# Weight chunk, small loads and tail transposes issued at other places in the start of an attention-plus-ReGLU kernel

## The chip, the cores and the metric

The kernel runs on one core of a Trainium2 chip. The metric is the device time of one execution in microseconds. Times differ a little from run to run and between chips, so every kernel was timed in turns with the kernel before on the same chip. The profile shows one of the executions, and its span is some 1.7 us shorter than the time of the same run. That execution need not be a typical one: the profiles of the kernel after, e5, e8, e9 and e10 fell on the fastest run of their kernel, those of e2, e6 and e7 on the slowest. Where a time in microseconds is given beside a ratio, the ratio is the one to trust.

## The reference, cut to what matters

```python
# q, k, v: (8, 8, 576, 64); beacon_k, beacon_v: (8, 8, 16, 64): 16 extra keys seen by every query
scores = scale * np.matmul(q, k_all.transpose(0, 1, 3, 2))      # causal on the 576 own keys
a = softmax(scores)
x = (a @ v_all) reshaped to (4608, 512)
out = (np.maximum(x @ w_gate, 0) * (x @ w_val)) @ w_out         # 512 -> 1536 -> 512
```

So there are eight batches of attention, then a feed-forward part over 4608 rows. The kernel runs them interleaved: TensorE does scores and e·v of one batch between the matmuls of the feed-forward part for rows that are ready.

## The kernel before

Everything is planned on the host as a list of steps. Steps one to seven are batch one alone, then come four steps without attention, of which three do feed-forward work, then batch two. Actions are hung on a step: `between` (behind the first score matmuls), `mid` (behind the first exponential), `behind`, and `after` (at the end). Each engine runs what it is given in this order. In the code, batches and steps count from 0 and `s2` is 11, the first step of batch two.

```python
def load_rows(self, srcs, held=False):
    raw = self.raw["rows"] = stage.tile([P, d_model], FP32, name="raw")
    n = srcs.shape[1]
    if held:
        nc.gpsimd.memset(raw[:1, :1], 0.0)     # SyncE's load below must wait for GpSimd to get here
    nc.sync.dma_start(...)
...
mid[3] = lambda: load_w(wg, moe_w_gate, 256, 768, (0,))
after(3, lambda: load_w(wg, moe_w_gate, 256, 768, (1,)))
...
after(6, lambda: load_w(wv, moe_w_val, 256, 768))          # GpSimd, float32 to bf16 on the way
after(6, load_small)                                       # beacon, key tail, query tail of batch two
for n0 in (768, 1152):
    after(6, lambda n0=n0: load_w(wg, moe_w_gate, n0, n0 + 384))
    after(6, lambda n0=n0: load_w(wv, moe_w_val, n0, n0 + 384))
after(6, lambda: load_second(0))                           # four "quarters" (hwide) of batch two, GpSimd
after(7, lambda: load_second(1))                           # four more
for t in range(NKT):
    after(7, lambda t=t: second.load("v", t, t == 0))      # SyncE; v block 0 is held by a memset
for t in range(NKT):
    after(s2 - 1 + t // 2, lambda t=t: second.cast("v", t, pool))
after(s2 - 2, lambda: load_wo(0, 6))                       # GpSimd, 768 KB as landed
after(s2 - 1, lambda: load_wo(6, 12))
after(s2 - 3, lambda: cast_small(second))                  # VectorE casts the three small loads
after(s2 - 2, lambda: turn_small(second))                  # TensorE transposes them
mid[s2 - 1] = lambda: turn_two(second, 0, s_ps)            # TensorE transposes the first four quarters
between[s2 + 1] = lambda: turn_two(second, 1, f_ps)
```

Names, for the timelines below: `wg`, `wv` and `wo` are the gate, value and output weights, and L466, L475 and L485 their matmuls; `hT` is the product of gate and value that L485 reads. `e` holds exponentials (L378, ScalarE), GpSimd masks them (L386), and L420 is e·v. `raw` buffers take float32 rows from memory, and a cast brings them to bf16 (`half`, `hwide`). A quarter (`hwide`) is 256 rows of q or k for four of the eight heads; the tails are the last rows, which the quarters leave out. A hold is a memset by GpSimd that a load must wait for; a hole is time in which TensorE stands idle. The granted clock is the share of full speed that TensorE was allowed, 1.0 or 0.5.

## Time and profile before

| what | value | where it is read |
|---|---|---|
| time | 397.75 us median (397.14 to 399.54, 4 runs) | timed runs |
| span of the profile | 396.4 us | page |
| TensorE busy | 374.1 us, 94% | page, part 1 |
| first feed-forward matmul (L466) | 29.68 us | timeline |
| GpSimd's first issue of a 768-column chunk | 30.29 us | timeline |
| GpSimd's memset that opens the v hold | 46.64 us | timeline |
| cast of batch two's first v rows starts | 57.10 us | timeline |
| TensorE resumes with e·v of batch two | 59.73 us | timeline |

The timeline: start us, duration, engine, line, what it does, and in brackets how long the engine had stood idle and what released it. The prediction below shows the lines themselves.

### The profile page before, as it was taken

Reading aid. Unit: us, or ns where it says so; the run is one execution under the profiler, and the core shown is the slowest. Engines: PE = TensorE matmul, PEld = TensorE weight load, DVE = VectorE, ACT = ScalarE, POOL = GpSimd, SP = SyncE. Lnnn points to the kernel's source line nnn. Section 1 sums busy time; section 2 is a strip of 40 time slices with the busy share of each in tenths; the row PEclk is TensorE's granted clock in tenths of the full one; section 3 lists DMA queues with packets and bytes.
Section 4 is the critical chain, followed back from the end, with each engine's and each line's share of the span. In section 5 each row is a group of like instructions: output and inputs, shape, how many; then the busy total and the mean of one; then the engine's idle time right before and its main releaser. Section 6 shows DMA issues by size and latency. Waiting matters only on the chain.

```text
span 396.4 us, 10219 instructions
## 1 busy us (share of the span) xinstructions
PE 374.1 (94%) x4243; PEld 189.8 (48%) x4299; DVE 204.9 (52%) x344; ACT 192.2 (48%) x268; POOL 127.7 (32%) x221
## 2 busy tenths in 40 slices
PE   7889669999999999999999999999999999999995
PEld 3464334544455445544454545554555454444443
DVE  4685435644556756366636564556555654421320
ACT  4663155533755655455636653656365643322321
POOL 1577526521653445053505350526020200000000
PEclk9999698999999999999999999999999999999999
DMA  8969999967989999399629962796210011002002
GB/s 217 196 121 163 188 201 190 208 146 160 207 157 156 208 186 133 103 200 173 124 96 198 181 122 96 179 189 135 71 53 2 2 55 53 2 27 81 1 25 86
DMA packets 148131, 50.43 MB, mean 127 GB/s; under 512 B 133616, under 2 KB 143600, under 8 KB 148080
## 3 DMA queue, kind: packets, MB, share of 16 engines
q1 hardware_dynamic: 139024, 44.48, 54.9%
q0 software_dynamic: 9056, 5.24, 10.0%
q8 instruction: 35, 0.57, 0.6%
q14 instruction: 16, 0.13, 0.1%
HBM read 38.34 MB, written 9.44 MB: 121 GB/s over the span
## 4 chain that ended last, share of the span: by engine, by line
PE 72%; DMA 13%; issue 5%; SPq 4%; POOL 3%; ACT 1%; DVE 1%; POOLq 0%; ACTq 0%
PE f L485 19%; PE f L466 19%; PE s L475 11%; PE f L475 8%; PE s L370 6%; PE ab L420 6%; DMA raw<-in_q_dram 4%; DMA raw<-in_v_dram 4%; DMA raw<-in_k_dram 3%; PE os L420 2%; DMA kT<-half 2%; SPq L244 2%; SPq L281 1%; ACT e L378 1%; SPq L310 1%
## 5 line engine op out<-in xcount | busy, mean ns | idle before, releaser
L378 ACT ACTIVATE e<-s 128x1024 bf16<-128x1024 f32 (+2 forms) x112 | 104.9, 963 | 27.4 <-PE s L370 27.4
L466 PE MATMUL f<-xT,wg 128*128 128x512 bf16 x405 | 110.3, 383 | 2.3 <-DMA hwide<-in_k_dram 0.7
L469 ACT ACTIVATE g<-f 128x512 f32<-128x512 f32 x108 | 64.6, 598 | 87.7 <-PE f L466 78.8
L485 PE MATMUL f<-wo,hT 128*128 128x512 bf16 (+1 forms) x424 | 94.8, 373 | 1.6 <-issue 0.8
L386 POOL TENSOR_SCALAR_AFFINE_SELECT e<-e 128x512 bf16<-128x512 bf16 (+2 forms) x80 | 47.3, 603 | 150.7 <-ACT e L378 142.4
L432 DVE RECIPROCAL r<-os 128x80 f32<-128x80 f32 (+2 forms) x43 | 57.6, 1339 | 56.5 <-PE os L420 56.5
L477 DVE TENSOR_TENSOR hT<-g,s 128x512 bf16<-128x512 f32 x60 | 41.3, 688 | 69.0 <-PE s L475 67.9
L475 PEld LDWEIGHTS <-wv 128*128 128x128 bf16 x432 | 42.6, 99 | 53.1 <-issue 3.4
L485 PEld LDWEIGHTS <-hT 128*128 128x128 bf16 x444 | 41.9, 98 | 47.3
L466 PEld LDWEIGHTS <-wg 128*128 128x128 bf16 x432 | 39.7, 98 | 47.6 <-issue 2.1
L475 PE MATMUL s<-xT,wv 128*128 128x512 bf16 x238 | 62.3, 383 | 0.2
L488 ACT COPY ob<-f 128x512 f32<-128x512 f32 (+1 forms) x37 | 21.3, 575 | 73.9 <-PE f L485 69.1
L477 DVE TENSOR_TENSOR hT<-g,f 128x512 bf16<-128x512 f32 x48 | 33.0, 688 | 35.3 <-PE f L475 30.6
L475 PE MATMUL f<-xT,wv 128*128 128x512 bf16 x186 | 49.0, 381 | 0.7 <-ACT qT L301 0.2
L263 POOL CAST half<-raw 128x512 bf16<-128x512 f32 (+2 forms) x60 | 37.1, 633 | 25.3 <-DMA raw<-in_k_dram 9.3
L420 PE MATMUL ab<-e,v 128*32 128x80 bf16 (+4 forms) x1320 | 39.7, 235 | 3.4 <-POOL e L386 3.4
L370 PE MATMUL s<-qT,kT 64*128 64x80 bf16 (+3 forms) x704 | 36.0, 236 | 1.8 <-ACT e L378 1.1
L420 PEld LDWEIGHTS <-v 128*32 128x32 bf16 (+1 forms) x1408 | 26.7, 98 | 13.3 <-issue 7.9
L370 PEld LDWEIGHTS <-kT 64*128 64x128 bf16 x704 | 20.5, 97 | 25.8 <-issue 23.6
L420 PE MATMUL os<-e,ones 128*32 128x240 bf16 (+4 forms) x660 | 32.3, 234 | 0.0
L259 POOL CAST v<-raw 128x512 bf16<-128x512 f32 (+1 forms) x39 | 25.6, 662 | 15.1 <-DMA raw<-in_v_dram 14.4
L445 DVE TENSOR_TENSOR xT<-ab,r 128x480 bf16<-128x480 f32 (+2 forms) x45 | 25.0, 554 | 0.8
(68 smaller groups left out, 139.0 us busy)
## 6 DMA issues: line engine op xcount, KB each, us to landing
out_dram<-ob SPq DMA_DIRECT2D x35, 256.0 KB, 2.1
raw<-in_q_dram SPq DMA_DIRECT2D x25, 256.0 KB, 4.8
raw<-in_v_dram SPq DMA_DIRECT2D x24, 256.0 KB, 5.0
raw<-in_k_dram SPq DMA_DIRECT2D x19, 256.0 KB, 4.4
raw<-in_v_dram SPq DMA_DIRECT2D x8, 224.0 KB, 3.8
wo<-in_moe_w_out_dram POOLq DMA_DIRECT2D x2, 768.0 KB, 9.5
raw<-in_k_dram SPq DMA_DIRECT2D x6, 224.0 KB, 4.3
raw<-in_v_dram SPq DMA_DIRECT2D x8, 160.0 KB, 4.3
```

The costliest lines, as they stand in the source:

```text
L259: copy(self.v[:n, t].rearrange("p (h a d) -> p h a d", a=2, d=C), raw[:n].rearrange("p (h d a) -> p h a d", a=2, d=C))
L263: copy(h[:n], raw[:n])
L370: nc.tensor.matmul(self.s[:, a, c + j * n:c + (j + 1) * n], kT[rows, 2 * g + j, k0:k0 + P], qT[rows, 2 * g + j, q0:q0 + n], start=True, st ...
L378: nc.scalar.activation(e[:, :k * 4 * n].rearrange("p (k a x) -> p a k x", k=k, a=2), self.s[:, :, :k * 2 * n].rearrange("p a (k x) -> p a ...
L386: nc.gpsimd.affine_select(out=cols[:, :, :m], in_=cols[:, :, :m], pattern=[[0, 4], [1, m]], compare_op=ALU.is_ge, fill=0.0, base=base, cha ...
L420: nc.tensor.matmul(o[:, q0 - cq0:q0 - cq0 + n], w, e[:kr, 2 * (hh % 2) + hh // 2], start=(i == 0 and part != 1), stop=(i == self.last), sk ...
L432: nc.vector.reciprocal(self.r[:, :n], self.os[:, :n])
L466: nc.tensor.matmul(g[:, :n], wg[:, ki, nf * P:(nf + 1) * P], x[:, ki], start=(ki == 0), stop=(ki == KM - 1))
L469: nc.scalar.activation(gs[:, :n], g[:, :n], AF.Relu)
L475: nc.tensor.matmul(u[:, :n], wv[:, ki, nf * P:(nf + 1) * P], x[:, ki], start=(ki == 0), stop=(ki == KM - 1))
L477: nc.vector.tensor_mul(self.h[:, nf, c0:c1], gs[:, :n], u[:, :n])
L485: nc.tensor.matmul(o[:, n], self.h[:, nf, ms * P:(ms + 1) * P], wo[:, nf, n], start=(nf == 0), stop=(nf == NF - 1))
```

## The change

The intent: the second 256-to-768 chunk of the value weights is issued from the fourth step on, the small loads of batch two go without a hold, and the tails of batch one (its last 80 rows) are cast and transposed later, in a score bank, so that the copies of the last quarters need not wait for them. Some casts change engine to make room. The diff, with the dead `held` parameter of `load_rows` cut:

```diff
         def turn_next():
             turn_first("k", 0, 1, dve)()
             first.cast_quarter("k", 1, 0, dve)
-            warm_up(1, 256)
...
             held.pop()()
-            warm_up(1, 256)
             turn_first("k", 1, 0, dve)()
...
         def cast_last():
             for n in "kq":
                 first.cast_quarter(n, 1, 1, dve)
+
+        def turn_last():
+            for n in "kq":
+                turn_first(n, 1, 1, dve)()
             cast_tails(first, dve)
 
         def turn_first_tails():
-            ps = f_ps.tile([P, 2, NP, 80], BF16, name="f")
+            ps = s_ps.tile([P, 2, NP, 256], BF16, name="s")
...
-        between[2] = lambda: [turn_first(n, 1, 1, dve)() for n in "kq"]
-        behind[2] = turn_first_tails
-        after(2, lambda: [held.pop(0)() for _ in range(2)])
-        after(2, lambda: first.cast("v", 2, pool))
-        after(2, lambda: first.cast("v", 3, pool))
-        mid[3] = lambda: load_w(wg, moe_w_gate, 256, 768, (0,))
-        after(3, lambda: load_w(wg, moe_w_gate, 256, 768, (1,)))
-        after(4, lambda: first.cast("v", 4, dve))
-        after(4, lambda: cast_w(wg, raw_g, 256, 0, dve))
-        after(4, lambda: cast_w(wg, raw_g, 256, 1, pool))
-        after(5, lambda: cast_w(wv, raw_v, 256, 0, pool))
-        after(6, lambda: cast_w(wv, raw_v, 256, 1, pool))
-        after(6, lambda: load_w(wv, moe_w_val, 256, 768))
-
-        def load_small():
-            second.beacon = second.load_rows(beacon_k[1], True)
-            load_tails(second)
-
-        after(6, load_small)
+        between[2] = turn_last
+        between[3] = turn_first_tails
+        behind[3] = lambda: [held.pop(0)() for _ in range(2)]
+        after(1, lambda: first.cast("v", 2, pool))
+        after(1, lambda: first.cast("v", 3, pool))
+        mid[3] = lambda: load_w(wg, moe_w_gate, 256, 768)
+        after(3, lambda: load_w(wv, moe_w_val, 256, 768, (0,)))
+        after(4, lambda: first.cast("v", 4, pool))
+        mid[5] = lambda: [cast_w(wg, raw_g, 256, g, pool) for g in range(2)]
+        mid[6] = lambda: load_w(wv, moe_w_val, 256, 768, (1,))
+        after(6, lambda: [cast_w(wv, raw_v, 256, g, act) for g in range(2)])
+        second.beacon = second.load_rows(beacon_k[1])
+        load_tails(second)
```

More of the change, by code (lines that the diff above doesn't have):

```diff
@@ L303, in turn_quarter, with load_rows @@
                 ps.rearrange("a j r p -> a j p r"))
-        def load_rows(self, srcs, held=False):
+        def load_rows(self, srcs):
             raw = self.raw["rows"] = stage.tile([P, d_model], FP32, name="raw")
             n = srcs.shape[1]
-            if held:
-                nc.gpsimd.memset(raw[:1, :1], 0.0)
             nc.sync.dma_start(raw[:n].rearrange("p (h d) -> p h d", d=D),
@@ L630, in cast_last @@
                 first.cast_quarter(n, 1, 1, dve)
+        def turn_last():
+            for n in "kq":
+                turn_first(n, 1, 1, dve)()
             cast_tails(first, dve)
         def turn_first_tails():
-            ps = f_ps.tile([P, 2, NP, 80], BF16, name="f")
+            ps = s_ps.tile([P, 2, NP, 256], BF16, name="s")
             for x, (h, dst) in enumerate(zip(first.tails, (first.kT4, first.qT4))):
-                held.append(first.turn_rows(h, dst[:, :, :80], act, ps[:, x]))
+                held.append(first.turn_rows(h, dst[:, :, :80], act, ps[:, x, :, :80]))
         behind[1] = cast_last
-        between[2] = lambda: [turn_first(n, 1, 1, dve)() for n in "kq"]
-        behind[2] = turn_first_tails
-        after(2, lambda: [held.pop(0)() for _ in range(2)])
-        after(2, lambda: first.cast("v", 2, pool))
-        after(2, lambda: first.cast("v", 3, pool))
-        mid[3] = lambda: load_w(wg, moe_w_gate, 256, 768, (0,))
-        after(3, lambda: load_w(wg, moe_w_gate, 256, 768, (1,)))
-        after(4, lambda: first.cast("v", 4, dve))
-        after(4, lambda: cast_w(wg, raw_g, 256, 0, dve))
-        after(4, lambda: cast_w(wg, raw_g, 256, 1, pool))
-        after(5, lambda: cast_w(wv, raw_v, 256, 0, pool))
-        after(6, lambda: cast_w(wv, raw_v, 256, 1, pool))
-        after(6, lambda: load_w(wv, moe_w_val, 256, 768))
-        def load_small():
-            second.beacon = second.load_rows(beacon_k[1], True)
-            load_tails(second)
-        after(6, load_small)
+        between[2] = turn_last
[11 more added lines that the diff above has]
+        load_tails(second)
         for n0 in (768, 1152):
```

## The prediction

> **What bounds the kernel now.** I read the page first, for the shape of the whole run. In the page's 40 slices (9.9 us each) TensorE is full from the seventh on; the clock and DMA rows show where it is not.
>
> ```profile
> PE   7889669999999999999999999999999999999995
> PEclk9999698999999999999999999999999999999999
> DMA  8969999967989999399629962796210011002002
> ```
>
> Count digits: PE has 6, 6 in slices 5 and 6 (39.6 to 59.5 us), the clock has 6 and 8 in slices 5 and 7. DMA has its one early dip, a 6, in slice 3 (19.8 to 29.7 us), and is at 9 right after. So what the change can win lies before 64 us; after that the list of TensorE waits for 64 to 396 us holds only 1.0 us, all "issue". Anything gained early should reach the end, if the later transfers keep up.
>
> Next, the busy time by stretch, whose last three columns are granted clock, DMA share and GB/s:
>
> ```profile
> 21.00:24.00 3.00, 2.90 (x70) 1.97 (x65) 2.02 (x6) 2.22 (x3) 2.99 (x6) 1.00 0.43 95
> 24.00:30.00 6.00, 4.29 (x200) 3.42 (x201) 5.29 (x13) 3.77 (x5) 3.83 (x7) 1.00 0.60 86
> 36.00:42.00 6.00, 4.32 (x20) 1.84 (x19) 1.95 (x6) 1.20 (x2) 2.49 (x4) 1.00 1.29 197
> 42.00:50.00 8.00, 5.93 (x52) 3.38 (x53) 4.40 (x14) 1.20 (x2) 4.39 (x7) 0.58 1.68 185
> ```
>
> From 21 to 30 us DMA moves 86 to 95 GB/s, then 185 to 197. The queue is saturated in one stage and half empty in the stage before it. Third, the timeline around the TensorE holes:
>
> ```profile
> 16.02 0.46 DVE L317 CAST half<-raw 80x512 bf16<-80x512 f32 x1 [0.26 <-DMA raw<-in_q_dram]
> 17.13 0.69 PE L325 MATMUL f<-ident,half 80*128 80x80 bf16 x8 [1.26 <-DVE kT L301]
> ...
> 38.18 0.42 DVE L317 CAST half<-raw 64x512 bf16<-64x512 f32 x1 [1.25 <-DMA raw<-in_k_dram]
> 41.40 0.42 DVE L317 CAST half<-raw 64x512 bf16<-64x512 f32 x1 [2.79 <-DMA raw<-in_q_dram]
> 42.50 0.60 ACT L469 ACTIVATE g<-f 128x512 f32<-128x512 f32 x1 [4.14 <-DVE hT L477]
> 43.15 0.78 PE L325 MATMUL f<-ident,half 16*128 16x16 bf16 x12 [2.83 <-ACT g L469]
> 46.29 1.91 PE L475 MATMUL s<-xT,wv 128*128 128x512 bf16 x4
> ...
> 57.10 1.20 POOL L259 CAST v<-raw 128x512 bf16<-128x512 f32 x2 [9.60 <-DMA raw<-in_v_dram]
> 58.26 0.82 POOL L350 DMA_DIRECT2D wo<-in_moe_w_out_dram  x1
> 59.08 0.60 POOL L386 TENSOR_SCALAR_AFFINE_SELECT e<-e 128x448 bf16<-128x448 bf16 x1
> 59.73 0.39 PE L420 MATMUL ab<-e,v 128*32 128x240 bf16 x8 [3.12 <-POOL e L386]
> ```
>
> Three holes. **First**, at 15.9 to 17.1 us TensorE waits for VectorE, which sat waiting for the tails of batch one. **Second**, at 40.2 to 43.2 us: batch two's small rows (key tail, query tail) are late, VectorE waits for them in order, so the hT products behind them are late, ScalarE has no g buffer, and TensorE has no bank. Four matmuls then take 1.91 us instead of 1.03. **Third**, at 56.6 to 59.7 us: TensorE waits for a mask on GpSimd that stands behind the cast of batch two's first v rows, and that cast waited 9.60 us for its transfer. Fourth view, the queue of issues:
>
> ```profile
> SPq L244 <- POOL raw L241: 14.6, 1, 14.6
> SPq L310 <- POOL raw L309: 10.8, 1, 10.8
> ```
>
> SyncE stood still for 10.8 us before the small loads and 14.6 us before v, because a one-element GpSimd memset holds each buffer. The small loads could have gone at 19.4 us, when SyncE's last weight issue ended.
>
> **What the Trainium skill says.** "DMA: Bandwidth & Descriptors", Issuing engines are not separate DMA queues: transfers issued anywhere run on the same 16 engines and interleave. The trace agrees: the 128 KB query tail, issued by SyncE at 31.48 us among GpSimd's weight chunks, took 9.9 us. "TensorE: Matmul & The Clock Gate", Architectural detail: VectorE and ScalarE queues are strictly first in, first out. The trace agrees: the hT product at 41.74 us runs only behind the 2.79 us wait of L317. The same page, What's actually happening: an idle TensorE falls to half clock after an idle window of about 3.4 us. The trace shows the fall after holes of 2.9 and 3.1 us; granted clock 0.58 in 42 to 50 us. "Perfetto Trace Analysis", DMA Instruction — SWDGE: a GpSimd DMA's row ends with descriptor generation, not with the data. So I read landings from the DMA issues in narrow windows: the 0.72 us rows land 4 to 10 us after issue.
>
> **The change part by part.**
>
> Tails of batch one. Their casts leave the place ahead of the kT and qT copies (0.67 + 0.67 us at 16.40 and 17.00), and their transposes get a score bank one step later. The two transposes of the last quarters end near 15.1 us, so the copies can run at about 15.0 to 16.3 and the first e·v group at about 15.8 (after the score matmuls of 15.26) instead of 17.74; v rows 0 and 1 were cast by 15.48. The eight tail transposes (0.6 us) come back in step four, and ScalarE's two tail copies (0.43 + 0.43) now stand between two exponentials. ScalarE then does one exponential per 1.02 us; following it from 17.45, the last one ends at about 27.1 instead of 28.31. Gain here: about **1.2 us**. The warm-up matmuls taken out (two of 0.4 us) filled time in which TensorE waited for VectorE casts; I give them 0.
>
> Casts moved. v block 4 and one wg half go from VectorE (0.41 each) to GpSimd (0.62 each), both wv halves from GpSimd (0.61 each) to ScalarE after its last exponential (0.62 each, its row for a cast of this shape). They end near 28.4, before wv is first read at about 29.4. GpSimd's total hardly moves: 0.
>
> Weight chunk two. The first half of wv[256:768] is issued at about 23.6 and the second at about 27.3, instead of both at 28.82. Each is 256 KB, in time for their use at about 32.8 (a lone one landed in 4.0 us).
>
> Small loads. 32 + 128 + 128 KB move from 30.4 us to 19.5. So 0.29 + 0.26 MB leave the saturated stretch; at about 190 GB/s (the narrow windows: 192 KB chunks land 1.0 us apart) that is 2.9 us. And GpSimd starts the stream earlier: its first 768-column wg issue goes from 30.29 to about 28.1, as it has 1.2 us from the exponentials, and two wv issues fewer but one at 27.3 there. By landings: that chunk landed at 36.4 (30.29 + 6.1), and should at 28.1 + 4.0 + 0.4 = 32.5; seven more at 1.0 us end at 39.5 against 45.3; the first hwide quarter lands at 40.3 against 46.1 (36.93 + 9.2). Shift **5.8 us**.
>
> Second hole. VectorE has no wait left at L317, so the hole of 2.9 us and the slow matmuls (eight at 1.87 + 1.91 against 2 × 0.86 by spacing, 2.1 us) go. TensorE reaches the quarter transposes at 48.13 − 1.2 − 2.9 − 0.6 (the wait for hT behind it) − 2.1 = about 41.4; the four quarters land at 40.3 to 42.6. Nearly no wait. TensorE is **6 to 7 us** ahead here.
>
> Third hole. This sets the end. SyncE's v loads go when GpSimd reaches its memset, behind the eighth hwide issue. In the trace every hwide issue from 36.93 on follows, by 0.3 to 0.6 us, the landing of the GpSimd transfer eight places before (36.4, 37.8, 40.2, 41.5, ...): eight in flight at most. After the change those landings are 32.5 to 39.5, so the eighth issue goes near 40.3 and the memset near 41.2 instead of 46.64. The v transfer beside the remaining hwide and wo traffic, which are as deep as before, still takes some 9.8 us: 51.4 instead of 56.96. Casts, wo issue and mask behind it are unchanged, 2.7 us: TensorE resumes at about 54.2 instead of 59.73, having been ready since about 50. So 5.5 of the 6.5 us of TensorE's lead survives, the hole grows from 3.1 to about 4.5 us, and its cold restart (60.5 to 63.5) stays. From there TensorE is full, and SyncE's batch-three loads follow the same v issue, so they shift with it.
>
> Sum: 397.4 − 5.5 = **391.9 us**.
>
> **Rivals.**
>
> A: the v loads do not move with the rest. They are still behind a hold, and share the engines with 1.5 MB of wo. For: TensorE's third hole ends on them and on nothing else. Against: the hold opens behind transfers that all come earlier. If only the 2.9 us of bytes counts: 394.5.
>
> B: TensorE bound, all holes lower. If v lands sooner after its issue (its 9.83 us is mostly queueing) the full lead of TensorE is kept, and less cold time: 397.4 − 7 to 8.5 = 389 to 390.4. For: 12 us of idle and cold time lie between 24 and 64 us. Against: the hold stays in.
>
> C: the start gets worse. The tails' copies delay exponentials on ScalarE, the score bank used by them delays a score tile, the wg casts on GpSimd stand ahead of a mask. For: ScalarE is nearly back to back from 11.61 to 15.52. Against: it has idle gaps of 0.5 to 0.9 us before each later group. If the start loses 1.5 us instead of winning 1.2: about 394.6.
>
> D: transfers hidden anyway, nothing changes: 397. Against: the chain of waits runs through the query tail for 9.89 us and v for 9.83.
>
> **Range and chances.** A and C set the upper end, 394.6; B the lower, 389.5. Faster by over 2% needs under 389.4, which is B at its best: 0.09. Slower by over 2% needs 405.3, and no mechanism above reaches it: 0.01. Within 2%: 0.90.
>
> **What would show it.** Right: no L317 wait of VectorE after 30 us; the small loads issued near 19.5; first hwide transfer landing near 40; memset near 41; v cast near 51.5; TensorE's hole before the first e·v of batch two still there, 4 us or more. First e·v of batch one near 15.8, first L466 near 28.4. Wrong: the eighth hwide issue later than 43.5, a mask of the first batch late on GpSimd, or new TensorE waits after 64 us, which would say that the later loads bind.

## The result and the profile after

The kernel after took 392.91 us (median, 392.56 to 393.27, 4 runs) against 397.75 us. The ratio is 0.9871, with a 95% interval of 0.9836 to 0.9906. A ratio here is the mean time of one kernel's fast runs over the mean of the other's fast runs in the same rounds, so it is not quite the quotient of the medians. The time fell by 1.3%, well clear of noise and within the 2% called "same". The span of the profile fell from 396.4 to 390.8 us.

The rows of the page of the kernel after (40 slices of 9.8 us; TensorE busy, granted clock, DMA busy, in tenths):

```profile
PE   6989859999999999999999999999999999999995
PEclk9999969999999999999999999999999999999999
DMA  8999999777995997399439943995200011002002
```

The DMA dip in the third slice is filled. TensorE's pair of sixes has become an eight and a five, and of two slices with a low clock one is left. So one of the two later holes is nearly gone and the other has got worse. The busy time by stretch says the same; the last three columns are clock, DMA share and GB/s:

```profile
21.00:24.00 3.00, 2.22 (x96) 1.85 (x92) 1.79 (x4) 2.46 (x4) 2.99 (x6) 1.00 1.00 167
24.00:30.00 6.00, 5.24 (x137) 2.87 (x134) 4.21 (x10) 3.28 (x6) 6.00 (x10) 1.00 1.05 160
42.00:50.00 8.00, 6.72 (x79) 3.51 (x80) 3.06 (x5) 4.12 (x7) 0.00 (x0) 1.00 1.37 196
50.00:60.00 10.00, 5.61 (x59) 2.58 (x64) 3.87 (x5) 3.73 (x6) 6.85 (x12) 0.66 1.02 189
```

Between 21 and 30 us the engines now move 160 to 167 GB/s instead of 86 to 95. The low clock has moved from 42 to 50 us (0.58 before) to 50 to 60 us (0.66). The timeline of the kernel after, at the places of the three holes:

```profile
15.37 0.59 PE L418 MATMUL ab<-e,v 128*32 128x240 bf16 x8
16.98 0.71 PE L323 MATMUL s<-ident,half 80*128 80x80 bf16 x8
17.62 0.47 PE L418 MATMUL f<-e,v 128*32 128x240 bf16 x8
...
33.70 1.08 DVE L315 CAST half<-raw 16x512 bf16<-16x512 f32 x3
37.43 0.59 PE L323 MATMUL f<-ident,half 16*128 16x16 bf16 x12
40.59 0.41 PE L300 MATMUL s<-ident,hwide 128*64 128x128 bf16 x8 [0.36 <-DMA hwide<-in_k_dram]
...
41.09 0.09 POOL L241 MEMSET raw<- 1x1 f32 x1
51.50 1.25 POOL L259 CAST v<-raw 128x512 bf16<-128x512 f32 x2 [9.54 <-DMA raw<-in_v_dram]
53.52 0.59 POOL L384 TENSOR_SCALAR_AFFINE_SELECT e<-e 128x448 bf16<-128x448 bf16 x1
54.16 0.59 PE L418 MATMUL ab<-e,v 128*32 128x240 bf16 x8 [4.38 <-POOL e L384]
```

Line numbers are two lower than before (L420 is now L418). The first hole is closed: the e·v group that began at 17.75 us begins at 15.37, and the tail transposes come behind it. The second is closed too: VectorE casts the three small loads in one go at 33.70, with nothing to wait for, and TensorE is at the quarters at 40.59 instead of 48.13, there waiting 0.3 to 0.4 us for each of the four (1.4 us in all). The third has grown from 3.12 to 4.38 us. TensorE comes 7.5 us earlier to the quarters and only 5.6 us earlier out of the third hole: 59.73 to 54.16. That 5.6 us is the whole difference of the spans.

### The profile page after: what moved, and what is told of

Read it like the earlier page. It is cut to its first block, busy times and chain, and to the rows that moved or that the text cites. A ratio compares the mean times of both kernels' runs of the same rounds, so it can differ in the third digit from the quotient of the medians.

```text
span 390.8 us, 10215 instructions
## 1 busy us (share of the span) xinstructions
PE 370.8 (95%) x4241; PEld 187.9 (48%) x4297; DVE 204.3 (52%) x342; ACT 192.9 (49%) x270; POOL 127.9 (33%) x220
## 4 chain that ended last, share of the span: by engine, by line
PE 90%; DMA 3%; ACT 2%; issue 2%; POOL 1%; DVE 1%; SPq 0%; POOLq 0%; DVEq 0%; ACTq 0%
PE f L483 24%; PE f L464 23%; PE s L473 13%; PE f L473 10%; PE s L368 8%; PE ab L418 7%; PE os L418 3%; DMA raw<-in_v_dram 3%; ACT e L376 1%; DMA wide<-in_q_dram 1%; PE f L300 1%; PE f L418 0%; POOL v L259 0%; POOL hwide L289 0%; PE s L418 0%
## 5 line engine op out<-in xcount | busy, mean ns | idle before, releaser
L483 PE MATMUL f<-wo,hT 128*128 128x512 bf16 (+1 forms) x424 | 94.8, 373 | 1.6 <-issue 0.8
L475 DVE TENSOR_TENSOR hT<-g,s 128x512 bf16<-128x512 f32 x60 | 41.2, 687 | 66.6 <-PE s L473 65.5
L483 PEld LDWEIGHTS <-hT 128*128 128x128 bf16 x444 | 41.9, 98 | 47.3
L473 PE MATMUL s<-xT,wv 128*128 128x512 bf16 x238 | 61.5, 379 | 0.2
L418 PE MATMUL ab<-e,v 128*32 128x80 bf16 (+4 forms) x1320 | 39.4, 234 | 4.4 <-POOL e L384 4.4
L259 POOL CAST v<-raw 128x512 bf16<-128x512 f32 (+1 forms) x40 | 26.9, 676 | 20.4 <-DMA raw<-in_v_dram 18.4
L418 PEld LDWEIGHTS <-v 128*32 128x32 bf16 (+1 forms) x1408 | 26.6, 97 | 14.1 <-issue 7.1
L418 PE MATMUL os<-e,ones 128*32 128x240 bf16 (+4 forms) x660 | 32.3, 233 | 0.0
```

The costliest lines, as they stand in the source:

```text
L259: copy(self.v[:n, t].rearrange("p (h a d) -> p h a d", a=2, d=C), raw[:n].rearrange("p (h d a) -> p h a d", a=2, d=C))
L418: nc.tensor.matmul(o[:, q0 - cq0:q0 - cq0 + n], w, e[:kr, 2 * (hh % 2) + hh // 2], start=(i == 0 and part != 1), stop=(i == self.last), sk ...
L473: nc.tensor.matmul(u[:, :n], wv[:, ki, nf * P:(nf + 1) * P], x[:, ki], start=(ki == 0), stop=(ki == KM - 1))
L475: nc.vector.tensor_mul(self.h[:, nf, c0:c1], gs[:, :n], u[:, :n])
L483: nc.tensor.matmul(o[:, n], self.h[:, nf, ms * P:(ms + 1) * P], wo[:, nf, n], start=(nf == 0), stop=(nf == NF - 1))
```

## The experiments

The theory under test is the prediction's. The end is set by the third hole. It ends when batch two's first v rows have landed; they land some 10 us after GpSimd's memset; and the memset stands behind eight quarters, each of which waits for an earlier GpSimd transfer to land. So whatever is taken out of that stream of transfers, or lets it start earlier, moves the end; TensorE's own holes in front of it do not. The main rival is that every microsecond of hole taken from TensorE before 64 us is kept.

Each run gives a profile; their moments are gathered here, in us. "Chunks" is GpSimd's first 768-column issue, "length" is memset less chunks, "rest" is the span less the moment at which TensorE resumes.

| kernel | first gate matmul | chunks | memset | length | v cast | TensorE resumes | span | rest |
|---|---|---|---|---|---|---|---|---|
| before | 29.68 | 30.29 | 46.64 | 16.35 | 57.10 | 59.73 | 396.4 | 336.7 |
| after | 26.88 | 26.62 | 41.09 | 14.47 | 51.50 | 54.16 | 390.8 | 336.6 |
| e1 | 29.94 | 30.51 | 44.84 | 14.33 | 55.29 | 57.96 | 395.6 | 337.6 |
| e2 | 30.19 | 30.11 | 45.93 | 15.82 | 56.57 | 59.27 | 396.3 | 337.0 |
| e3 | 28.18 | 28.26 | 44.66 | 16.40 | 55.08 | 57.71 | 395.0 | 337.3 |
| e8 | 26.56 | 26.33 | 41.73 | 15.40 | 52.16 | 54.90 | 391.6 | 336.7 |
| e5 | 26.72 | 26.45 | 40.57 | 14.12 | 47.09 | 49.95 | 388.5 | 338.5 |

In all rows but the last, v cast less memset is 10.4 to 10.6 us and the rest is 336.6 to 337.6 us, while the moments before it move by up to 5.6 us. That is the theory in one table: from the memset on, these kernels are the same to within 1.0 us.

How far two profiles of one stream differ can be read too. The kernel after was profiled twice (memset 41.09 and 41.35 us), and so was e5 (40.57 and 42.72): the start varies by up to 2 us, for a reason given below. The length varies less. Six profiles have the stream of the kernel after unchanged (after, e4, e5, e9, e10, e11); it is 14.1 to 14.5 us in five and 15.2 in e11. So a difference of length under some 1 us, as in e2 and e8, is not settled by one profile.

### e1: the small loads alone

```diff
-        def load_small():
-            second.beacon = second.load_rows(beacon_k[1], True)
-            load_tails(second)
-
-        after(6, load_small)
+        second.beacon = second.load_rows(beacon_k[1])
+        load_tails(second)
```
(on the kernel before)

> The kernel before, with the three small loads of batch two issued early and without a hold, nothing else. Stream theory (the end is set by the third hole, which ends 10 us after the v hold opens, and the hold opens when GpSimd's weight and quarter transfers have landed): 0.29 MB leave a stream of about 190 GB/s, so the GpSimd memset of the v hold goes from 46.64 to about 45.1 us, the v cast from 57.1 to about 55.6, and the time is 1.5 us less, about 396.2. The second hole (VectorE at L317) is gone all the same, and TensorE stands at the quarters or in a longer third hole instead. Hole rival (every us of TensorE hole taken away before 64 us is kept): 2.9 us of hole, 0.6 of the wait behind it and 2.1 us of slow matmuls go, about 392.1.

Measured: 397.22 us median (6 runs) beside 397.61 of the kernel before; ratio 0.9953 (0.9909 to 0.9998). From the timeline of e1:

```profile
36.78 1.09 DVE L317 CAST half<-raw 16x512 bf16<-16x512 f32 x3
44.33 0.41 PE L300 MATMUL s<-ident,hwide 128*64 128x128 bf16 x8 [1.02 <-DMA hwide<-in_k_dram]
44.84 0.09 POOL L241 MEMSET raw<- 1x1 f32 x1
55.29 1.25 POOL L259 CAST v<-raw 128x512 bf16<-128x512 f32 x2 [9.60 <-DMA raw<-in_v_dram]
57.96 0.59 PE L420 MATMUL ab<-e,v 128*32 128x240 bf16 x8 [3.15 <-POOL e L386]
```

The second hole is gone and TensorE is at the quarters 3.8 us earlier (48.13 to 44.33). Yet the memset is 1.80 us earlier, the v cast 1.81 and TensorE's return 1.77. The other 2.0 us do not go into a longer wait for v, since the third hole is as long as before (3.15 against 3.12 us). They go on the way to it: 0.7 us at the quarters, which have not all landed, and 1.2 us in eight matmuls behind them, which ran at the low clock. The rival's 5.6 us would be a ratio of about 0.986, outside the interval. This run refutes the rival. TensorE's arrival at the third hole moved by as much as v (1.8 us), so the times alone do not say which of the two ends it. The timeline does: TensorE has been idle for 3.15 us when the mask comes.

### e2: the weight chunk alone

```diff
-        mid[3] = lambda: load_w(wg, moe_w_gate, 256, 768, (0,))
-        after(3, lambda: load_w(wg, moe_w_gate, 256, 768, (1,)))
+        mid[3] = lambda: load_w(wg, moe_w_gate, 256, 768)
+        after(3, lambda: load_w(wv, moe_w_val, 256, 768, (0,)))
+        mid[6] = lambda: load_w(wv, moe_w_val, 256, 768, (1,))
...
-        after(6, lambda: load_w(wv, moe_w_val, 256, 768))
```
(on the kernel before)

> The kernel before, with only the second weight chunk moved (both wg halves in the fourth step, wv's halves behind it and in the seventh). Stream theory: about half of the 0.5 MB of wv and one or two GpSimd issues of 0.72 us leave the saturated stretch, so the memset comes 1.5 to 2 us earlier and the time is 1.5 to 2 us less, about 396; the wait of VectorE for the query tail stays, some 1.5 us earlier, and the third hole stays near 3 us. Hole rival: only what the second hole loses, about 1.5 us too; so this run tells little between the two, but gives the size of this part.

Measured: 396.99 us median (6 runs), ratio 0.9947 (0.9903 to 0.9991), but in the profile the memset came only 0.7 us earlier, where 1.5 to 2 were expected. GpSimd's chunk issues began at 30.11 us, 0.2 us earlier than before: the late half of wv and a cast still stood in front of them. The length shrank by 0.5 us. VectorE waited 3.26 us for the query tail, as before, and the third hole was 4.08 us instead of the 3 that I expected to stay. Alone, this part is small; its size is not settled better than "0.7 us in a profile, 2 us by a ratio with an interval of the same size".

### e3: the start alone

The kernel after, with the weight chunk and the held small loads put back as before.

> The kernel after, with the weight chunk and the held small loads as before: only the start is changed (tails, casts, warm-ups). First L466 at about 27 us as in the kernel after (29.68 before). Stream theory: GpSimd comes to its run of issues 1.5 to 2.5 us sooner and the whole stream with it, memset at about 44.5, time about 395.5. VectorE still waits for the tails. Hole rival: the 2.8 us of the start are kept in full, 395. A third theory, that the start is swallowed by the wait for v: 397.5.

Measured: 395.40 us median (6 runs), ratio 0.9927 (0.9882 to 0.9972). First L466 at 28.18 us, not 27. The chunks begin 2.03 us earlier, the length is unchanged (16.40 against 16.35), the memset comes 1.98 us earlier and TensorE returns 2.02 us earlier. It reached the third hole 2.7 us earlier (53.91 against 56.61), so here the wait for v did grow, to 3.80 us. So the start is worth what it moves the stream. That the start is swallowed by the wait for v is refuted.

### e8: the small loads held again, in the kernel after

```diff
-        second.beacon = second.load_rows(beacon_k[1])
-        load_tails(second)
+        def load_small():
+            second.beacon = second.load_rows(beacon_k[1], True)
+            load_tails(second)
+
+        after(6, load_small)
```

> The kernel after, with only the small loads held as before. Stream theory: 0.29 MB back in the stream, memset from 41.1 to about 42.6, time 1.5 us more than the kernel after, about 394.4; the second hole comes back (VectorE waits 3 to 5 us at the casts of the small rows), but the third hole gets shorter by as much, less 1.5 us. Hole rival: the second hole adds itself, 4 to 5.6 us more, about 397.5.

Measured: 393.94 us median (6 runs), ratio 0.9894 (0.9851 to 0.9937), against 0.9871 for the kernel after. The memset is 0.64 us later than in the kernel after and TensorE's return 0.74: less than the 1.5 expected, and no more than two profiles differ by anyway. The rival's 4 to 5.6 us would be a ratio of about 0.997 to 1.001, outside the interval. VectorE waits again:

```profile
36.76 0.42 DVE L317 CAST half<-raw 64x512 bf16<-64x512 f32 x1 [2.35 <-DMA raw<-in_q_dram]
```

I had the wrong place for what absorbs it. The third hole was not shorter (4.48 us); instead TensorE, coming later to the quarters, found them nearly landed, and waited 0.4 us there instead of 1.4. The second hole itself cost hardly anything in this kernel, since another wait for the same stream lies right behind it.

### e4: the warm-up matmuls put back

```diff
             first.cast_quarter("k", 1, 0, dve)
+            warm_up(1, 256)
...
             held.pop()()
+            warm_up(1, 256)
```
(on the kernel after)

> The kernel after, with the two 256-column warm-up matmuls of the first step put back. The prediction gave them 0. If they cost their place, the first matrix of exponentials after the first (the run of four) starts 0.2 to 0.4 us later than 11.19 us and the whole start with it, memset about 41.4, time at most 0.4 us more. If on the other hand they keep TensorE warm, the clock rises earlier than at 17.6 us and the start is no slower. Either way within 0.5 us of the kernel after, about 393.

Measured: 393.50 us median (4 runs), ratio 0.9867 (0.9812 to 0.9922), the same as the kernel after. In this profile the run of exponentials began earlier than in the kernel after (10.05 against 11.19 us), but the first gate matmul came later, at 28.23 us. On the way TensorE waited for GpSimd's cast of v rows,

```profile
15.48 0.41 PE L418 MATMUL ab<-e,v 128*32 128x128 bf16 x8 [1.36 <-POOL v L259]
```

and the granted clock fell to 0.5 at about 15.1 us, inside this wait, and stayed there until about 21.9. No difference of time can be charged to the two matmuls within these intervals; the 0 of the prediction stands.

### e5, e10: wo one step later

```diff
-        after(s2 - 2, lambda: load_wo(0, 6))
-        after(s2 - 1, lambda: load_wo(6, 12))
+        after(s2 - 1, lambda: load_wo(0, 6))
+        after(s2, lambda: load_wo(6, 12))
```
(on the kernel after)

> The kernel after, with both halves of wo issued one step later, the first behind the casts of v rows 0 and 1 instead of at the v hold. Sharing theory (v takes 10 us because 0.77 MB of wo and the last quarters run on the same engines beside it): the memset stays at 41.1, the v cast comes 3 to 4 us sooner, at 47.5 to 48.5; TensorE resumes near 50 to 51 with hardly any third hole (it is ready at 49.8) and without the cold restart; time 3.5 to 5 us less than the kernel after, about 388.5, if wo still lands before the first L483 at about 61 us. Rival (v is slow by its own queue or packets, or by SyncE's issue): v cast stays at 51 to 51.5 and the time is that of the kernel after or worse by a wait for wo.

Measured: 391.78 us median (4 runs), ratio 0.9833 (0.9773 to 0.9893). The timeline of e5:

```profile
40.57 0.09 POOL L241 MEMSET raw<- 1x1 f32 x1
47.09 1.44 POOL L259 CAST v<-raw 128x512 bf16<-128x512 f32 x2 [6.43 <-DMA raw<-in_v_dram]
49.95 0.39 PE L418 MATMUL ab<-e,v 128*32 128x240 bf16 x8 [0.54 <-POOL e L384]
63.19 1.46 PE L483 MATMUL f<-wo,hT 128*128 128x512 bf16 x6 [1.25 <-DMA wo<-in_moe_w_out_dram]
```

With wo out of the way, v is there 6.5 us after the memset instead of 10.4, as the sharing theory says, the third hole shrinks from 4.38 to 0.54 us, and the clock does not fall (granted clock 1.0 over the run). TensorE resumes 4.2 us earlier than in the kernel after. But the span is only 2.3 us shorter. Most of the 1.9 us of difference can be seen. TensorE waits 1.25 us before the second half of the first L483, where wo is now the late one, 0.97 us for a mask at 94.4 us and 0.86 us for a query transpose at 118.7 us, and the kernel after has none of these three. Against that, the full clock saves about 1.6 us behind the third hole (4.51 us from the return to the second group of gate matmuls, 6.14 in the kernel after). Some 0.5 us stay unexplained. The bound has moved in part to later transfers.

To see whether this is real, e10 ran the same kernel again beside the kernel after.

> The kernel of e5 again in the rounds of the kernel after: is its gain of 1.1 us (medians of different rounds) or 2.3 us (spans) real? Sharing theory: v cast about 6.5 us behind the memset instead of 10.4, no third hole, and part of the 4.2 us given back at a wait for wo (1.25 us at the first L483) and at later loads; 1 to 2.5 us less than the kernel after in the same rounds. Rival: no difference beyond the noise of 0.5 us.

Measured: 392.04 us median (6 runs), ratio 0.9824 (0.9785 to 0.9864), where the kernel after, in the same rounds, had 394.16 us and 0.9876. So it is about 0.5%, 2.1 us, faster. The two intervals overlap a little, but both carry the noise of the kernel before; taken directly, the means of the two differ by 2.0 us (95% interval 0.8 to 3.1, worked out from these rounds), so the gain is real. In the profile of e10 v came 6.2 us after the memset, and the wait for wo was 1.1 us.

### e6, e7: the v hold opened earlier

```diff
-        after(7, lambda: load_second(1))
         for t in range(NKT):
             after(7, lambda t=t: second.load("v", t, t == 0))
+        after(7, lambda: load_second(1))
```
(e6 on the kernel after, e7 on e5)

> The kernel after, with the v hold opened before the second four quarters are issued and not behind them. Memset near 37 instead of 41.1. Theory: v still shares the engines, with more bytes ahead of it, so its cast comes 2 to 3.5 us sooner, about 48 to 49.5; the second four quarters land later by what v takes, near 50, and TensorE then waits for them before the e.v group; net 1.5 to 3 us less than the kernel after, 390 to 391.5. Rival (only the order changes, the last of both lands when it did): no gain, 393.

Measured for e6: 394.55 us (4 runs), ratio 0.988 (0.9825 to 0.9936): no gain. The memset came at 36.28 us and the first e·v of batch two at 52.11 us, 2.1 us sooner than in the kernel after, but a later v block became the late one, and its cast stands in front of a mask:

```profile
59.91 0.63 POOL L259 CAST v<-raw 128x512 bf16<-128x512 f32 x1 [6.46 <-DMA raw<-in_v_dram]
61.13 0.59 PE L418 MATMUL ab<-e,v 128*32 128x240 bf16 x8 [5.35 <-POOL e L384]
```

The hole has moved to the next e·v group and is 5.35 us long. I had expected the wait at the second four quarters. With wo moved as well this hole goes:

> Both of the edits of e5 and e6. If the third hole is all transfers in the shared engines, v and the quarters are there before TensorE wants them at 48 to 50 us, and it is no better than e5 alone by more than 1 us: about 388. If the engines are already the bound in e5, the two together give 387.

Measured for e7: 391.80 us (4 runs), ratio 0.9815 (0.9762 to 0.9868), no better than e5 within the intervals. Its v block 0 was there by 44.62 us, but the first e·v came only at 53.40: TensorE now waited 3.3 us in all for the first four quarters, which v's transfer now runs beside, and the matmuls behind them ran at the low clock.

### e9, e11: the kernel after once more, and wo's second half sooner

> The kernel after once more, unchanged, to stand in the same rounds as the next two, and to see how far the start varies. In the ten profiles so far the first L466 came at 26.5 to 27.1 us where the clock had risen by about 17.6 us, at 28.2 where it had not (starts of the kernel after), and at 29.7 to 30.2 with the start of before. [...]this run has its first L466 at either 26.5 to 27.1 or near 28.2. Memset 41 to 42, third hole 4 to 4.5 us, time 393 within 0.7.

Measured for e9: 394.16 us median (7 runs), ratio 0.9876 (0.9838 to 0.9914), confirming the first 0.9871. First gate matmul at 27.08, memset 41.35, TensorE resumes 54.37, a third hole of 4.34 us. The expectation about the start was too narrow for its companions: e10 had its first gate matmul at 29.22 us and e11 at 27.47.

e11 is e5 with this:

```diff
-        after(s2, lambda: load_wo(6, 12))
+        mid[s2] = lambda: load_wo(6, 12)
```

> The kernel of e5 with the second half of wo issued behind the first mask of its step instead of behind the casts of v rows 2 and 3: at about 49.9 us instead of 52.4. If the wait of 1.25 us before the first L483 came from that issue, it goes, and the time is about 1 us less than e5, 390 to 391. If wo is bound by the shared engines, it lands only a little sooner and batch three's loads come later instead: the same as e5.

Measured: 392.28 us median (6 runs), ratio 0.9822 (0.9782 to 0.9863), the same as e10. The second half of wo went out 8.7 us behind the memset instead of 11.6 in e10 (51.15 against 54.27 us), and the wait for it was 0.76 us instead of 1.11. A mask on GpSimd at 96.8 us cost 1.45 us; the same mask cost 0.56 in e10 and 0.97 in e5, which are one kernel, so it varies by itself. The time is that of the second of the two expectations. That what is won at wo is lost at a later load fits, but is not shown.

## Why the prediction was right, and where its steps were off

The predicted 391.9 us was 1.0 us under the measured 392.91, inside the range, and the predicted fall of 5.5 us (from 397.4 us, where these rounds gave 397.75) is 5.6 us by the spans, 4.8 by the medians, and 5.1 by the ratio, with an interval of 3.7 to 6.5.

**The third hole sets the end: right, and shown.** Predicted: memset near 41.2, v cast 51.4, TensorE back at 54.2, hole about 4.5 us. Measured: 41.09, 51.50, 54.16, 4.38 us. e1 and e8 refute that every hole of TensorE is kept in the time, and e5 shows that some 4 of the 10 us from the memset to the v cast come from wo beside it, as they fall to 6.5 us when wo is elsewhere. What the remaining 6.5 us are was not tested.

**The sum was right by two errors that cancel.** For the stream, I had the chunks begin at 28.1 us and the memset 13.1 us behind them. Measured were 26.62 and 14.47 us. The stream began 3.7 us earlier than before instead of 2.2, and became 1.9 us shorter instead of 3.3. The first term failed at the step "the last one ends at about 27.1": the last exponential of batch one ended at 25.4 us. The second failed at "seven more at 1.0 us": the eight 192 KB chunks landed 1.14 us apart on average, the first 5.2 us after its issue and not 4.4. The 1.0 was read from the last four chunks of the kernel before; over all eight they landed 1.29 us apart there.

**The start was mis-sized: 1.2 us predicted, 2.8 measured, and much of the excess is luck.** The step that failed is one I never wrote out: I kept TensorE at half clock until 22.6 us, as in the profile before. Eight 240-column e·v matmuls took 0.59 us at 15.37 us in the kernel after and 0.47 at 17.62; before, the same matmuls still took 0.59 at 19.35 and a 256-column group got to 0.44 only at 22.64. The clock is read from these durations, because its record says 1.00 throughout both starts; in e7 and e8, where the record does show the rise from 0.5 (at 15.7 and 14.9 us), the same 240 columns go from 0.59 to 0.39 us.

Over the ten profiles with the new start, the clock was up by about 17.6 us in seven, with the first gate matmul at 26.46 to 27.47 us, and not before about 21.9 in three (e3, e4, e10), with 28.18 to 29.22. The three profiles with the old start, all at the low clock, have 29.68 to 30.19. So the prediction's 28.4 is about right for a run whose clock stays low, and the rest came with the clock. The new start gave both, and seven of ten against none of three is too few to call the earlier rise an effect of the change; this was not tested by itself. The first cast also began 0.58 us earlier than before (4.42 against 5.00 us), ahead of any edited instruction. With the old start that gains nothing: e1 and e2 began as early, and VectorE then waited 1.5 and 2.1 us for the tails, so their gate matmuls came no earlier.

**The small loads.** Predicted: 0.29 MB at 190 GB/s, 1.5 us. By the length of the stream, 2.0 us (e1) and 0.9 us (e8). **The weight chunk**: 0.26 MB, 1.4 us predicted; 0.5 us of length in e2. So the bytes alone were a fair estimate for the small loads in e1; the other two figures lie within what profiles of one stream differ by, and the chunk's share stays open.

**The second hole** went as predicted, with TensorE at the quarters at 40.59 us against about 41.4; the lead is 7.5 us, above the 6 to 7, as the start gave more. The 2.1 us for the slow matmuls set durations against spacings; by spacing alone (44.63 to 48.13) they are 1.8. "Nearly no wait" was wrong by 1.4 us, which the third hole, 4.38 us long, took up.

**Rivals.** D, nothing changes, and C, the start gets worse, did not come. A, the v loads lag, did not come in the kernel after. B, in which the v transfer gets quicker than 9.8 us, did not come in the kernel after either; e5 made it come, and even then the time fell by about half of what TensorE had won, as later transfers took over.

**What stays open.** The three parts' ratios, 0.9953, 0.9947 and 0.9927, multiply to 0.983, below the 0.987 of the whole; each interval is wide enough to hide the difference. Why the chunks land 1.14 us apart and not 1.0 is not known. Of the 1.9 us that e5 gives back, some 0.5 are not accounted for. The 2.7 us of casts, wo issue and mask on GpSimd between the landing of v and TensorE's return, which are on the chain, were not touched by any run.

## What to carry to other kernels

Look for the wait that ends last, and ask what has to move for it to move; an earlier hole taken away on the busiest engine was given back here before that wait or in it, beyond what the transfers themselves had moved. In e1, 2.0 of 3.8 us went at the quarters and at the low clock; in the kernel after TensorE reached the third hole 6.8 us earlier and left it 5.6 us earlier. A hold that orders transfers ties a load to the landing of everything in front of it, so half-idle DMA time before such a stream is worth filling. When a transfer is late, see which other transfer shares the engines and can wait, and expect the gain to be partly taken by that one.

## What the Trainium skill lacked or had wrong

- "DMA: Bandwidth & Descriptors" says that transfers share 16 engines, but has no figure for what a load then takes. Here v rows (256 KB) were cast 10.4 us after the hold opened with 768 KB of wo beside them and 6.0 to 6.5 us without; the 128 KB query tail took 9.9 us among the weight chunks and 4.0 us in the quiet stretch at 19.7 us.
- No page tells of a limit on GpSimd transfers in flight. In the kernel before and the kernel after every quarter of batch two was issued 0.3 to 0.6 us behind the landing of the GpSimd transfer eight places earlier. Whether this is the chip's or the program's own semaphores was not tested.
- "TensorE: Matmul & The Clock Gate", What's actually happening, ties the rise of the clock to about 3.4 us of activity in a free-running window. The runs agree in kind: the clock was up by about 17.6 us or not before about 21.9 us in profiles of the same start, which moved the first gate matmul between 26.46 and 29.22 us.
- The same section gives an idle window of about 3.4 us for the fall. Here the clock also fell after holes of 2.9 and 3.1 us with slack around them, and in e4 inside a hole of 1.36 us, with TensorE busy for 2.1 of the 3.4 us before the fall; it did not fall after the hole of 0.5 us in e5.
